# A gated linear attention and a bilinear feed-forward: the same steps in another written order

## The chip, the core and the metric

The kernel runs on one core of one Trainium2 chip. The metric is the device time of one execution in microseconds (us). Of the kernel before there are three runs: 193.24, 193.31 and 193.69 us, median 193.31. A profile was taken of one more execution.

A core has five engines with a queue of instructions each: TensorE (PE in the profile; its weight loads are listed as PEld), VectorE (DVE), ScalarE (ACT), GpSimd (POOL) and SyncE (SP). Each works through its own queue in order, and waits on semaphores for the others. DMA transfers are issued from a queue, here GpSimd's and SyncE's (and once ScalarE's), and run beside the engines. Memory on the core is SBUF, and PSUM for what TensorE writes.

## The reference

There are 4 batches, 8 heads, 768 positions and a head width of 48. The first half is a recurrence over the positions, with a gate alpha for each element:

```python
for t in range(S):
    state = alpha[:, :, t, :, None] * state + np.einsum('bhd,bhe->bhde', k[:, :, t], v[:, :, t])
    y[:, :, t] = np.einsum('bhd,bhde->bhe', q[:, :, t], state)
```

The result, seen as 3072 tokens of 384 values, goes through a bilinear feed-forward of inner width 1536:

```python
a = x @ w_a
b = x @ w_b
return (a * b @ w_out).astype(np.float32)
```

Inputs and output are float32.

## The kernel before

**Tiling.** The 768 positions are cut into three stretches of 256 and the four batches into two pairs: six *chunks*, numbered 0 to 5 (chunk c holds stretch c // 2 of batches c % 2 * 2 and the next). The two batches of a chunk are its *units* u = 0 and 1. A partition holds two neighbouring positions r = 0, 1, and the 128 partitions of a unit are two halves g = 0 and 1 of 64, between which a state is carried.

**The steps.** The kernel is a list of steps, `PROGRAM`, written out by hand or by a planner outside the kernel; an interpreter at its end calls one small function for each step, in the order of the list. Nothing reorders it later: the order of the list is, engine by engine, the order of each queue, and what a step waits for follows from the tiles and the PSUM banks that it touches. A line of the list begins with the chunk; the letter at a step's end names the engine where there is a choice: V VectorE, S ScalarE, P GpSimd, Y SyncE. A step's last number is mostly its PSUM bank, of eight (0 to 7); wide results take that bank and the next. The steps, in the order in which a chunk needs them:

- `ld a|k|q|v`: loads of alpha, k, q, v. `W a|b`, `Wo`: loads of the feed-forward's weights, in column pieces. `T`: a transposing DMA by SyncE of chunks 2 to 5's scaled q and k of a unit; `dr`, `dl`: the last gates of each half written out and read back by DMA. `st`, `stc`: stores of the output.
- `ln`: logarithm of alpha (ScalarE, line 510). `l2`, `l2s`: sum of it over a pair of positions. `H`, `L`, `R`: splits of that sum into parts for exact products. `B`, `A2`, `AQ`: the running sum over positions as matmuls (lines 545 and 546, 592, 587). `dk`, `de`: the sum over a half as matmuls (654) and its exponential. `ra`, `lv`: correction within a pair (599, 606).
- `E x i`, `E x b`: exponentials of the sum with both signs (621). `mk`, `mq`: k and q times them, into `QKp` (632).
- `C`, `Ce` (chunks 0 and 1): transposes on TensorE (692) and the copy of the result out of PSUM into `kqT` (914 on ScalarE, 916 on VectorE and GpSimd). `Tr` (chunks 2 to 5): a reordering copy of `T`'s keys into `kp`.
- `v`, `vs`: values copied into `vx`, once straight (725, 727) and once with their quarters of 32 partitions swapped. `vs u g e` makes the two copies of 32 x 384 elements of a unit's half g on engine e.
- `K`, `K2`: what keys and values add to the state (748, 761). `k`: the new state (775, or 778 and 779). `D`: the scores (793). `M` masks them out of PSUM on VectorE (802); `Mc` copies them on ScalarE (806) and `Mm` masks the copy on VectorE (810).
- `SB`, `SA`, `Y`: the output of the attention, from the carried state and from the masked scores (822). `X`: its copy to `xT` (858, 860).
- `a f w`, `b f w`: three matmuls (877) for block f of 12 of the feed-forward, over half of the chunk's tokens (w = 0 or 1; 256 columns) or all (`*`; 512). I call one such step a pass. `as`: `a` copied to SBUF by ScalarE (883). `pr`: times `b`, on VectorE (891), which frees both banks.
- `o m h`: half of the last product for 128 tokens (899), `oc` the same in smaller pieces (910). `ot`: its copy to SBUF (914 or 916), then `st`.

**What lies where.** GpSimd's queue holds loads between its other work, and waits of that work hold back the loads behind it. SyncE's queue holds loads, stores and `T` of chunks 2 to 5; a `T` that waits for VectorE holds back the loads behind it. Chunk c + 1's attention is laid between chunk c's feed-forward passes, so that TensorE has passes to do while the other engines prepare.

Of the kernel before, what the change touches and what calls it, by code (L numbers as in the profile page):

```python
# [17 lines left out]
0: cm 0; c1; cz 0 b P; ci; ld a 0b Y; c1a; ld a 0a Y; ln 0b; cu; cz 1 b P; fill 7 0; cu2 V; cz 0 q V; cus; ld k 0b Y; ld k 0a Y; B 0b 2; ln 0a  # L18
# [21 lines left out]
0: as 4 1; pr 4 1; pr 10 *; a 9 * 2; a 3 1 1; Wo 6 12  # L40
1: L 1 V
2: ld a * P
1: ld v 1 P; E 0 b
0: b 8 * 7
1: E 0 i
0: as 3 1; as 9 *
2: ld q * P
1: lv 0 k V; mk 0 V
0: b 3 1 1; pr 3 1
1: dk * 4; de *  # L50
0: b 9 * 1
# [72 lines left out]
1: a 5 1 5; pr 2 1; a 9 0 4; b 9 0 6; b 5 1 7; as 6 1; pr 6 1
2: lv 0 k P; mk 0 V; T 0
3: v 0 S
1: as 9 0; pr 9 0; a 3 1 1; b 3 1 3; as 5 1; pr 5 1
2: K2 * * 4 5
3: vs 0 0 V; ra 0
1: b 9 1 6; as 3 1  # L130
4: ld a * Y
1: pr 3 1; a 9 1 1; o 2 0 3; o 2 1 -
2: k * 0 V; k * 1 V
3: vs 0 1 S
0: st 1 Y
1: b 0 1 7
2: Tr 1 V; v 0 S; vs 0 1 V
3: ld q * Y
1: b 7 1 4; as 0 1; pr 0 1; as 9 1; as 1 1
3: ld k * Y  # L140
1: b 8 1 2; a 7 1 5; ot 2 S
2: v 1 S; vs 1 1 P
3: l2s 0 P
1: as 7 1
4: ld k * Y
3: v 1 V
1: pr 9 1; b 1 1 3; pr 1 1; pr 7 1; a 11 1 0
# [12 lines left out]
2: SB 0 0; SB 1 2; D 0 1 6; Mc 0 1; Mm 1 0 V  # L160
1: o 3 0 5; o 3 1 -
2: vs 1 0 S
3: AQ 6
2: SA 0
1: ot 3 S; st 3 Y
0: st 2 Y
3: E 1 b; E 0 b; dr
4: ld q * Y
3: dl
2: SA 1  # L170
3: E 1 i
# [885 lines left out]
```

## Time and profile before

| | us |
|---|---|
| median of three runs | 193.31 |
| the profiled execution | 193.74 |
| its span, first to last instruction | 191.8 |
| TensorE busy | 184.5 |
| VectorE busy | 136.8 |
| ScalarE busy | 114.1 |
| GpSimd busy | 52.9 |

A row of the timeline gives the start, the duration, the engine, the line, the operation, output<-inputs by the names of the program, the shapes and how many like instructions were merged; in brackets stands how long the engine had been idle and what ended that. A row of a group gives, behind the bar, the busy time, the mean duration in ns, and the idle time ahead of them. Matmuls are pipelined: a mean duration is longer than the time from one start to the next. Issuing a DMA is shown on the engine whose queue issues it (SPq is SyncE's queue).

### The profile page before, as it was taken

The numbers are of one execution on the slowest core, as the hardware profiler recorded it, in microseconds if no ns is written. First come the engines' busy times: TensorE is split into PE (matmuls) and PEld (weight loads), VectorE is DVE, ScalarE is ACT, GpSimd is POOL, SyncE is SP. The second block draws the span as 40 slices with busy tenths as digits, with TensorE's granted clock in tenths as the row PEclk, the third lists the DMA queues.
The fourth block names the chain that finished last, engine by engine and source line by source line (L and its number), as shares of the span: only waits on it lengthen the run. The fifth ranks groups of instructions, "written<-read, shape, count | busy, mean of one in ns | idle before, by whom it ended". The sixth has DMA issues, their size and how long they took to land.

```text
span 191.8 us, 6128 instructions
## 1 busy us (share of the span) xinstructions
PE 184.5 (96%) x2597; PEld 115.2 (60%) x2613; DVE 136.8 (71%) x251; ACT 114.1 (59%) x216; POOL 52.9 (28%) x80
## 2 busy tenths in 40 slices
PE   7999999999999999999999999999999999999993
PEld 3987775666778876644446554556446555444562
DVE  2398887888998997689899996899085742234711
ACT  4446475797988888853867558775266151424321
POOL 8999506595424035000460000300030000000000
PEclk9999999999999999999999999999999999999999
DMA  5999999999994999989999988026812100210013
GB/s 137 267 221 213 254 249 239 241 265 269 252 207 86 84 205 281 257 240 156 200 296 191 180 123 201 4 82 86 177 6 82 46 3 0 82 41 3 0 68 137
DMA packets 64475, 29.41 MB, mean 153 GB/s; under 512 B 55760, under 2 KB 62816, under 8 KB 64448
## 3 DMA queue, kind: packets, MB, share of 16 engines
q1 hardware_dynamic: 46080, 16.34, 40.3%
q0 software_dynamic: 18224, 12.58, 38.0%
q8 instruction: 20, 0.33, 0.7%
q10 hardware_dynamic: 144, 0.10, 0.1%
q14 instruction: 7, 0.06, 0.1%
HBM read 25.98 MB, written 4.74 MB: 160 GB/s over the span
## 4 chain that ended last, share of the span: by engine, by line
PE 73%; DVE 12%; DMA 5%; issue 3%; ACT 3%; SPq 2%; DVEq 0%; ACTq 0%
PE psum L877 38%; PE psum L899 18%; DMA k_t<-in_k_dram 5%; PE psum L822 4%; DVE QKp L632 2%; DVE prod L891 2%; PE psum L528 2%; PE psum L692 2%; DVE vx L916 2%; PE psum L793 2%; SPq L932 1%; PE psum L748 1%; PE psum L545 1%; PE psum L910 1%; PE psum L546 1%
## 5 line engine op out<-in xcount | busy, mean ns | idle before, releaser
L877 PE MATMUL psum<-xT,wa_t 128*128 128x512 bf16 (+1 forms) x265 | 55.0, 336 | 0.6 <-DVE tmp L778 0.2
L877 PE MATMUL psum<-xT,wb_t 128*128 128x512 bf16 (+1 forms) x260 | 54.5, 335 | 0.9 <-DVE prod L891 0.3
L899 PE MATMUL psum<-wo_t,prod 128*128 128x384 bf16 x276 | 49.4, 326 | 0.0
L877 PEld LDWEIGHTS <-wa_t 128*128 128x128 bf16 x270 | 25.8, 98 | 20.6 <-issue 0.8
L877 PEld LDWEIGHTS <-wb_t 128*128 128x128 bf16 x270 | 25.5, 98 | 19.3 <-issue 0.9
L899 PEld LDWEIGHTS <-prod 128*128 128x128 bf16 x276 | 26.2, 98 | 17.6
L916 POOL COPY vx<-v_t 32x384 bf16<-32x384 bf16 x12 | 6.1, 508 | 49.8 <-ACT vx L725 40.9
L914 ACT ACTIVATE ot<-psum 128x384 f32<-128x384 f32 (+1 forms) x19 | 9.0, 472 | 11.3 <-PE psum L899 9.7
L806 ACT ACTIVATE m<-psum 128x768 bf16<-128x768 f32 x14 | 11.0, 810 | 2.9 <-PE psum L793 2.9
L606 POOL TENSOR_TENSOR q_t<-q_t,ra 128x384 f32<-128x384 f32 x4 | 4.0, 998 | 30.8 <-ACT ra L599 21.0
L916 DVE COPY ot<-psum 128x384 f32<-128x384 f32 x6 | 3.3, 557 | 11.2 <-PE psum L899 11.2
L510 ACT ACTIVATE la<-a_t 128x1536 f32<-128x1536 f32 (+2 forms) x9 | 9.5, 1054 | 2.9 <-DMA a_t<-in_alpha_dram 2.9
L858 ACT ACTIVATE xT<-psum 128x768 bf16<-128x768 f32 x10 | 7.9, 809 | 4.3 <-PE psum L822 4.3
L802 DVE TENSOR_TENSOR m<-psum,mask 128x768 bf16<-128x768 f32 x10 | 9.3, 951 | 1.3 <-PE psum L793 1.3
L632 DVE TENSOR_TENSOR QKp<-q_t,beta 128x768 bf16<-128x768 f32 x10 | 9.5, 954 | 0.6 <-DVE q_t L606 0.5
L632 DVE TENSOR_TENSOR QKp<-k_t,invb 128x768 bf16<-128x768 f32 x10 | 9.4, 953 | 0.2
L822 PE MATMUL psum<-m,vx 64*64 64x64 bf16 (+1 forms) x576 | 8.7, 205 | 0.2 <-issue 0.2
L503 POOL DMA_DIRECT2D v_t<-in_v_dram x8 | 8.5, 1063 | 0.0
L822 PEld LDWEIGHTS <-vx 64*64 64x64 bf16 x576 | 7.5, 108 | 0.6 <-issue 0.5
L725 ACT ACTIVATE vx<-v_t 128x768 bf16<-128x768 bf16 x9 | 7.6, 843 | 0.0
L822 PE MATMUL psum<-kqT,Sm 64*64 64x128 bf16 x144 | 7.6, 218 | 0.0
L914 ACT ACTIVATE vx<-v_t 32x384 bf16<-32x384 bf16 x14 | 7.3, 522 | 0.2
(278 smaller groups left out, 308.6 us busy)
## 6 DMA issues: line engine op xcount, KB each, us to landing
out_dram<-ot SPq DMA_DIRECT2D x23, 192.0 KB, 2.1
q_t<-in_q_dram SPq DMA_DIRECT2D x3, 768.0 KB, 6.2
k_t<-in_k_dram SPq DMA_DIRECT2D x3, 768.0 KB
a_t<-in_alpha_dram POOLq DMA_DIRECT2D x2, 768.0 KB, 11.3
v_t<-in_v_dram POOLq DMA_DIRECT2D x4, 384.0 KB, 11.1
a_t<-in_alpha_dram SPq DMA_DIRECT2D x2, 768.0 KB
a_t<-in_alpha_dram POOLq DMA_DIRECT2D x3, 384.0 KB, 7.8
k_t<-in_k_dram POOLq DMA_DIRECT2D x3, 384.0 KB, 6.9
```

The lines of the kernel that those rows point to most:

```text
L503: eng.dma_start(out=t[:, us, hs].rearrange("p b h r d -> p (b h) (r d)"), in_=src[ch.b0 + us.start:ch.b0 + us.stop, hs, ch.s * 2 * C:(ch.s ...
L510: nc.scalar.activation(out=ch.la[:, us, hs].rearrange("p b h r d -> p (b h r d)"), in_=ch.a[:, us, hs].rearrange("p b h r d -> p (b h r d) ...
L632: eng.tensor_mul(QKp[ch.c % 2][:, u, j, :, hs, :D], src[:, u, hs].rearrange("p h r d -> p r h d"), f)
L725: nc.scalar.activation(out=o_, in_=i_, func=AF.Copy)
L802: nc.vector.tensor_mul(m, x, maskn())
L806: nc.scalar.activation(out=m, in_=x, func=AF.Copy)
L822: nc.tensor.matmul(o, lhsT=lhsT, rhs=rhs, start=(g, c) not in begun, stop=False, skip_group_check=True)
L858: nc.scalar.activation(out=o_, in_=i_, func=AF.Copy)
L877: nc.tensor.matmul(p, lhsT=(wa_t, wb_t)[w][:, kk, f * 128:(f + 1) * 128], rhs=ch.xT[:, kk, us, :], start=(kk == 0), stop=(kk == KT - 1))
L899: nc.tensor.matmul(op, lhsT=ch.prod[:, f, at:at + C], rhs=wo_t[:, f, :], start=(f == 0), stop=(f == NFF - 1))
L914: nc.scalar.activation(out=o_, in_=i_, func=AF.Copy)
L916: eng.tensor_copy(o_, i_)
```

## The change

The list holds the same 872 steps, and each queue issues the same loads. What differs is the order of the steps, the PSUM banks, and the engine of 45 of them. By engine, the swaps `vs` go from 11 on VectorE, 7 on ScalarE and 6 on GpSimd to 10, 11 and 3. GpSimd issues its loads in the old order. On SyncE the loads keep their order among themselves, and some stores stand elsewhere between them. `l2 0` of chunk 1 moves from VectorE to GpSimd, `Ce 0 1` of chunk 0 from VectorE to ScalarE, `Ce 0 0` and `Ce 1 1` of chunk 1 the other way, and some `lv`, `v`, `Tr`, `ot` and `X` change engine in both directions. The work on each engine in all stays nearly as it is.

The start of the list, chunk 0 and the first steps of chunk 1:

```diff
-0: B 0a 0; ld q 0b Y; E 0b i; mk 0b V; dk 0 4; E 0b b; mq 0b V; C 0 1 5; E 0a i; mk 0a V; E 0a b; fill 2 0; ld v 0 P; ld q 0a Y; mq 0a V; de 0; Ce 0 1 V; ld a 1 P
-0: ln 1; cs 0 m P; C 0 0 1; Ce 0 0 V; ld k 1 P; K 0 0 2; k 0 0 V; ld q 1 P; cm 1; D 0 1 4; M 0 1; D 0 0 0; M 0 0; v 0 S; vs 0 1 V; SB 0 2; vs 0 0 V; B 1a 6
-0: E 1a b; mq 1a V; E 1a i; mk 1a V; B 1b 4; W b 0 256; E 1b b; mq 1b V; dk 1 0; E 1b i; de 1; C 1 0 1; cz 0 v P; Y 0; SA 0; mk 1b V; C 1 1 0; Ce 1 0 V
-0: Ce 1 1 V; D 1 0 4; ld v 1 P; K 1 0 1; K 1 1 6; X 0 S; v 1 S; Mc 1 0; D 1 1 2; Mc 1 1; W a 256 768; a 3 0 0; a 4 0 7; k 1 0 V; cz 1 q P; as 4 0; vs 1 0 V; a 5 0 1
-0: W a 0 256; a 0 0 4; as 5 0; vs 1 1 V; Mm 1 0 V; SB 1 2; W b 256 768; b 4 0 5; Mm 1 1 V; cs 1 m P; b 3 0 1; a 1 0 7
-1: ld a 0 P; ld a 1 P
-0: k 1 1 V; a 2 0 6; as 2 0; pr 4 0; K 0 1 5; k 0 1 V; SA 1; Y 1; b 2 0 6; pr 2 0; b 1 0 5; as 1 0; pr 1 0; b 5 0 7; pr 5 0; W a 768 1536; X 1 S; c2 P
-0: b 2 1 2; a 2 1 3; W b 768 1536; a 1 1 5
...
+0: ln 0a; ld v 0 P; E 0b i; mk 0b V; E 0b b; mq 0b V; B 0a 0; E 0a i; ld q 0a Y; ld a 1 P; dk 0 2; cs 0 m P; ld k 1 P; ld q 1 P; E 0a b; cm 1; W b 0 256; C 0 1 3
+0: Ce 0 1 S; fill 2 0; mk 0a V; cz 0 v P; ld v 1 P; mq 0a V; C 0 0 1; Ce 0 0 V; K 0 0 0; W a 256 768; de 0; D 0 1 2; cz 1 q P; D 0 0 4; W a 0 256; W b 256 768; ln 1; cs 1 m P
+1: ld a 0 P
+0: k 0 0 V; v 0 S; vs 0 0 S; M 0 1; SB 0 0; B 1a 6
+1: ld a 1 P
+0: M 0 0; vs 0 1 V; B 1b 2; E 1a b; W a 768 1536; mq 1a V; dk 1 4; E 1a i; mk 1a V; C 1 0 5; c2 P; Y 0; SA 0; W b 768 1536
+1: ld q 0 P
+0: E 1b i; mk 1b V; K 1 0 6; E 1b b; v 1 S; mq 1b V; C 1 1 7
+1: ld k 0 P; ld v 0 P
+0: Ce 1 0 V; D 1 0 2; K 1 1 5; X 0 S; a 3 0 0; vs 1 0 V; de 1; Mc 1 0; as 3 0; a 4 0 4; as 4 0; a 5 0 1; Ce 1 1 V; k 1 0 V; D 1 1 2; k 1 1 V; SB 1 6; vs 1 1 V
+0: a 1 0 0; Mm 1 0 V; b 4 0 4; pr 4 0; Mc 1 1; a 2 0 5; as 2 0; Mm 1 1 V
+1: ln 0
+0: b 3 0 2; a 0 0 3; b 2 0 5
+1: l2 0 P
+0: b 5 0 4; pr 3 0; as 5 0; pr 5 0; SA 1; Y 1; X 1 S; pr 2 0; K 0 1 2; b 0 0 1
 1: ld q 1 P
...
+0: b 1 0 4; a 3 1 5; a 2 1 6; Wo 0 6; b 2 1 7; as 0 0
```

Further on, the places in SyncE's queue of `T 0` of chunk 2, a store of chunk 0 and the loads behind them, and VectorE's steps around chunk 2's `Y`s:

```diff
+0: st 1 Y
...
+2: lv 0 k P; mk 0 V; T 0
...
+4: ld a * Y
...
+3: ld q * Y; ld k * Y
...
-2: lv 0 k P; mk 0 V; T 0
...
-4: ld a * Y
...
-0: st 1 Y
...
-3: ld q * Y
...
-3: ld k * Y
...
-2: SB 0 0; SB 1 2; D 0 1 6; Mc 0 1; Mm 1 0 V
-1: o 3 0 5; o 3 1 -
-2: vs 1 0 S
-3: AQ 6
-2: SA 0
...
-3: E 1 b; E 0 b; dr
...
-2: Mm 0 0 V; Mm 0 1 V; Y 1; X 1 V
...
-2: Y 0; X 0 S
+1: o 3 1 -; ot 3 S; st 3 Y
+2: Mm 1 0 V
+3: R 1
+2: vs 0 1 V; Mm 0 0 V
+3: AQ 6; E 0 b
+2: SA 0; vs 1 0 V; Y 1
+3: E 1 b
+2: vs 0 0 V
...
+2: Mm 0 1 V; Y 0; SA 1
+3: lv 0 q V; mq 0 V
...
+2: X 0 S
...
+2: X 1 S; a 3 * 7; b 0 * 2
```

In the last 60 us the passes, `T` and `dr` of chunk 5 stand in another order too; the last four `oc` groups and the last stores stand in the same order.

More of the change, by code (lines that the diff above doesn't have):

```diff
@@ L47 @@
+1: H 0 V; L 0 V; ra 0
+0: b 0 1 3; pr 0 0; as 1 0; pr 1 0
+1: ln 1; ra 1
+0: k 0 1 V
+1: l2 1 V; H 1 V; L 1 V
+0: as 2 1; a 0 1 0; as 0 1; as 3 1; b 3 1 1; a 6 * 4
+1: A2 0 2; E 0 i
+0: pr 0 1
+1: lv 0 q P
+0: pr 2 1; b 1 1 0
+1: ld k 1 P
+0: a 10 * 5; Wo 6 12; as 6 *
+2: ld a * P
+0: a 7 * 6; pr 3 1; b 6 * 3; pr 6 *; b 10 * 1; as 10 *; pr 10 *
+1: E 0 b; mq 0 V
+0: b 7 * 7; as 7 *; pr 7 *
+1: ld v 1 P; dk * 2
+0: a 1 1 1
 2: ld q * P
+1: lv 1 q P; lv 1 k P; de *
+2: ld k * P
 1: lv 0 k V; mk 0 V
-0: b 3 1 1; pr 3 1
@@ new lines @@
+3: ld v * P
+0: cz 1 v P; b 11 * 3; a 4 1 5; as 1 1; as 11 *; pr 11 *; a 5 1 1
+1: A2 1 2
+0: pr 1 1
+1: E 1 i
+0: b 8 * 6
+1: E 1 b
+0: b 4 1 4; c3 P
+3: ld a * P
+1: mq 1 V; v 0 S
+0: a 8 * 7
+1: C 0 0 0; Ce 0 0 V
+0: b 5 1 2; o 2 0 3; as 5 1; as 4 1; pr 4 1; cs 1 0 P; as 8 *
+1: vs 0 0 S; C 0 1 7; D 0 0 0
+0: pr 5 1; pr 8 *
+1: K2 0 0 2 4; k 0 0 V
+0: o 3 0 5
+1: Mc 0 0; mk 1 V; Ce 0 1 S; vs 0 1 S
+0: o 1 0 2
+1: k 0 1 V; SB 0 0
+2: ln *
+1: D 0 1 6
+0: o 3 1 -
+1: M 0 1; Mm 0 0 V; v 1 S; C 1 0 4; Ce 1 0 V; C 1 1 6; Ce 1 1 V
@@ new lines @@
+3: vs 0 0 S
+1: b 4 1 2
+2: Tr 0 V
+1: b 11 1 3; o 0 0 0; pr 4 1
+2: D 1 0 4; Mc 1 0; D 0 0 6; Mc 0 0
+1: b 1 1 1; o 0 1 -; pr 11 1
+3: R 0
+2: SB 1 2; SB 0 4; D 0 1 6
+1: pr 1 1; o 3 0 1
+2: Mc 0 1
+1: o 3 1 -; ot 3 S; st 3 Y
[6 more added lines that the diff above has]
+2: vs 0 0 V
+0: st 2 Y; cs 0 0 P
+2: Mm 0 1 V; Y 0; SA 1
+3: lv 0 q V; mq 0 V
+1: o 1 0 1; o 1 1 -
+3: E 1 i; lv 0 k V
+2: X 0 S
+3: lv 1 q V; mq 1 V
+2: X 1 S; a 3 * 7; b 0 * 2
@@ L196 @@
+3: E 0 i
+4: ln *; ra 1; l2 0 P
+2: b 1 * 3
+3: dr
+2: a 0 * 6; as 0 *
+1: ot 1 S
+3: lv 1 k V; mk 1 V
+2: a 1 * 4; b 11 * 5
+3: mk 0 V
+4: ld q * Y
+1: ot 0 S
+2: pr 0 *; b 3 * 6; as 3 *
+3: v 1 V; vs 1 0 V
+4: l2s 0 V
+2: as 1 *; pr 1 *
+3: dl
+2: pr 3 *; a 6 * 0; a 11 * 1; a 7 * 4
+3: K2 * * 2 7
+2: as 11 *
+3: k * 0 V; k * 1 V
+1: st 2 Y
+2: pr 11 *; b 9 * 1; a 5 * 3
+3: vs 0 1 S
+2: as 5 *
+3: T 0
+2: a 2 * 6; b 2 * 2; as 2 *; pr 2 *; b 5 * 3; pr 5 *
 3: T 1
-4: lv 0 k V
-2: as 3 *; as 4 *; pr 4 *; a 9 * 2; as 9 *; b 9 * 5
+2: a 4 * 6
@@ L355 @@
-5: oc 1 0 1 -; otc 1 0 S; stc 1 0 Y
+2: b 10 * 1; pr 10 *
+3: D 0 1 2
+4: lv 0 q P
+3: Mc 0 1
+4: lv 1 q V
+3: D 0 0 4; Mc 0 0; D 1 0 6; M 1 0; Mm 0 1 V
+2: o 0 0 0; o 0 1 -
+3: SB 1 2; SB 0 4
+4: l2s 1 P
+3: D 1 1 6; Mc 1 1
+2: o 2 0 1; o 2 1 -
+5: ln *
+3: Mm 0 0 V
+2: ot 2 S
+4: R 0; R 1; AQ 6; E 0 b; E 1 i; lv 1 k V
+3: Mm 1 1 V
+5: l2s 0 V
+4: mq 0 V
+3: vs 1 1 P
+4: E 0 i
+3: SA 1; SA 0; Y 0; X 0 S; Y 1; X 1 S
+4: E 1 b
+5: l2 0 V
+2: st 2 Y
+1: st 1 Y
+2: o 1 0 1; o 1 1 -
+4: lv 0 k P; mk 0 V
@@ new lines @@
+5: l2s 1 V; R 0
+3: a 2 * 2
+4: mq 1 V
+3: as 2 *; b 9 * 3
+4: ld v * P
+5: R 1; ra 1
+4: T 0
+3: a 8 * 4; as 8 *
+4: dr
+3: b 2 * 2
+4: v 0 V; mk 1 V
+3: a 4 * 5; as 4 *; a 9 * 4
+4: T 1; v 1 S; vs 1 0 S
+3: b 4 * 6; pr 4 *; b 8 * 5; pr 8 *; pr 2 *
+5: lv 1 q V
+3: b 11 * 7
+4: Tr 0 V
+3: a 6 * 6; as 6 *; b 6 * 5; pr 6 *
+2: ot 1 S
+5: ra 0
+3: as 9 *
+5: lv 0 q P
+3: a 11 * 2; as 11 *; pr 9 *
+2: ot 0 V
+3: a 1 * 6; pr 11 *; b 1 * 1; as 1 *; pr 1 *
+4: vs 1 1 S
+3: a 3 * 4; b 3 * 5; as 3 *; pr 3 *; a 5 * 0; as 5 *
@@ new lines @@
+5: lv 0 k P; AQ 2; E 0 b; E 0 i
+4: dl
+5: ld v * P
+4: D 0 1 6; vs 0 1 P; K * 0 1; D 0 0 4; M 0 0; k * 0 V; Tr 1 S
+2: st 1 Y
+4: vs 0 0 S
+5: E 1 b
+4: M 0 1
+2: o 3 0 0; o 3 1 -; ot 3 S
+3: b 5 * 2; pr 5 *
+5: mk 0 V; mq 0 V
+3: a 7 * 1
+5: dr
+4: D 1 1 4; SB 0 6
+5: E 1 i
+4: Mc 1 1
+3: a 0 * 0
+5: lv 1 k V
+3: b 0 * 2; as 0 *; pr 0 *; b 7 * 3; a 10 * 0
+4: D 1 0 4
+3: as 7 *
+4: Y 0; Mc 1 0; SB 1 1; SA 0
+3: pr 7 *; b 10 * 3
+5: mq 1 V; mk 1 V
+3: o 0 0 4
+5: T 0
+3: as 10 *; pr 10 *
+5: Tr 0 V
@@ new lines @@
+3: o 3 0 0; o 1 0 3
+5: T 1
+3: o 0 1 -
+5: K * 0 5
+4: Mm 1 0 V; Mm 1 1 V; Y 1; SA 1; X 1 V
+5: dl
+3: ot 0 V; o 1 1 -; o 3 1 -
+4: X 0 S; a 6 * 1; as 6 *; b 6 * 2; a 3 * 4
+5: k * 0 V; Tr 1 S
+4: pr 6 *
+2: st 3 Y
+4: a 0 * 1; as 0 *; as 3 *
+3: ot 3 V
+4: a 4 * 2; b 3 * 0; pr 3 *
+3: o 2 0 1
+5: D 0 0 4; D 1 0 6; v 1 V; M 1 0
+2: st 0 Y
+3: ot 1 S
+5: vs 1 1 V
+4: as 4 *
+5: D 1 1 2; vs 1 0 S
+4: b 0 * 0
+3: o 2 1 -
+5: v 0 S; vs 0 1 P
+3: ot 2 S
+5: vs 0 0 V; Mc 0 0; Mm 0 0 V
+4: b 9 * 6
+5: Mc 1 1
```

376 lines of the change are left out of this document (93 added, 283 removed).

## The prediction

> **What bounds the kernel now.** I read the page first: its head, the slices and the shares of the chain.
>
> ```profile
> span 191.8 us, 6128 instructions
> PE 184.5 (96%) x2597; PEld 115.2 (60%) x2613; DVE 136.8 (71%) x251; ACT 114.1 (59%) x216; POOL 52.9 (28%) x80
> ...
> DVE  2398887888998997689899996899085742234711
> ...
> PEclk9999999999999999999999999999999999999999
> ...
> PE 73%; DVE 12%; DMA 5%; issue 3%; ACT 3%; SPq 2%; DVEq 0%; ACTq 0%
> ```
>
> TensorE is busy for 96% of the span at full granted clock. Both orders issue the same matmuls, so the change can move only what TensorE waits for: some idle time before the first matmul, and holes that VectorE's results, ScalarE's results or late loads leave. VectorE is at eight to nine tenths up to about the thirtieth slice (140 us) and slack afterwards, so I looked for holes in the first 100 us, by the timeline of each engine and the chain of waits. I compare the orders by landmarks: a place where equally much TensorE work lies behind. A pass is three matmuls with one weight block; a half-wide one (256 columns) takes 0.33 us in the timeline below (1.48 us for twelve matmuls, four passes, less the pipelined tail).
>
> **The change, part one: the start.** The stretch from 10 to 26 us, from the timelines of ScalarE, VectorE and TensorE:
>
> ```profile
> 10.50 0.84 ACT L510 ACTIVATE la<-a_t 128x768 f32<-128x768 f32 x1 [0.87 <-DMA a_t<-in_alpha_dram]
> 11.25 0.83 ACT L725 ACTIVATE vx<-v_t 128x768 bf16<-128x768 bf16 x1
> 13.63 0.87 ACT L621 ACTIVATE prod<-psum 128x384 f32<-128x384 f32 x2 [1.55 <-PE psum L546]
> 15.78 0.35 ACT L675 ACTIVATE bl<-psum 48x8 f32<-48x8 f32 x2
> ```
> ```profile
> 9.84 1.50 DVE L916 COPY kqT<-psum 128x1024 bf16<-128x1024 bf16 x2
> ...
> 11.51 1.81 DVE L802 TENSOR_TENSOR m<-psum,mask 128x768 bf16<-128x768 f32 x2
> 13.36 1.42 DVE L916 COPY vx<-v_t 32x384 bf16<-32x384 bf16 x4
> 14.80 0.56 DVE L632 TENSOR_TENSOR QKp<-q_t,prod 128x384 bf16<-128x384 f32 x1
> 15.28 0.55 DVE L632 TENSOR_TENSOR QKp<-k_t,prod 128x384 bf16<-128x384 f32 x1
> ...
> 18.97 1.71 DVE L916 COPY vx<-v_t 32x384 bf16<-32x384 bf16 x4
> ```
> ```profile
> 14.82 0.91 PE L654 MATMUL psum<-og,la 128*48 128x2 f32 x32
> 15.89 0.62 PE L692 MATMUL psum<-ident,QKp 128*128 128x128 bf16 x8 [0.15 <-DVE QKp L632]
> 16.44 0.72 PE L822 MATMUL psum<-m,vx 64*64 64x128 bf16 x48
> ...
> 22.80 0.49 PE L748 MATMUL psum<-v_t,QKp 64*64 64x48 bf16 x16 [0.26 <-DVE prod L891]
> ...
> 23.92 1.48 PE L877 MATMUL psum<-xT,wb_t 128*128 128x256 bf16 x12
> 25.24 0.82 PE L877 MATMUL psum<-xT,wa_t 128*128 128x256 bf16 x6
> ```
> ```profile
> L914 ACT ACTIVATE vx<-v_t 32x384 bf16<-32x384 bf16 x14 | 7.3, 522 | 0.2
> L916 DVE COPY vx<-v_t 32x384 bf16<-32x384 bf16 x22 | 6.6, 298 | 0.4
> ...
> L914 ACT ACTIVATE kqT<-psum 128x1024 bf16<-128x1024 bf16 x3 | 3.1, 1029 | 0.0
> ```
>
> The last fence is the list of groups by form: a swap is two copies, so 1.04 us on ScalarE and 0.60 on VectorE.
>
> ScalarE in the new order takes over `Ce 0 1` at 9.84 (1.03, to 10.87), then `de 0` (0.35, to 11.22), the logarithm (0.84, to 12.06), the cast (0.83, to 12.89), the swap (1.04, to 13.93) and the first exponential of 1a (half of 0.87, to 14.37), some 0.3 us later than now. VectorE has one swap instead of two: 13.32 plus half of 1.42 is 14.03; it waits for that exponential, and the two products of 1a end near 15.50 (0.48 us from start to start in the rows). TensorE's gate sums end at 15.73 (14.82 + 0.91), so the transposes `C 1 0` can start there, not at 15.89. The order after it (`Y 0`, `SA 0`, `K 1 0`, `C 1 1`) keeps TensorE fed while VectorE makes the products of 1b and `Ce 1 0`.
>
> The larger gain is at 22 us. Now the pass at 22.06 ends in 0.5 us, and `K 0 1` waits until 22.80 for bank 5 (`pr 4 0`). In the new order `K 0 1` stands behind `SA 1` and `Y 1`, with seven half-wide passes ahead of them; I followed each bank and found its `as` or `pr` done before it is asked for, `pr 4 0` by 0.4 us. That gives: `SB 1` done near 20.1, seven passes 2.3, `SA 1` and `Y 1` 0.9, `K 0 1` 0.3, two passes 0.65, together 24.25. Equal work lies before 25.24 now. Gain 1.0 us; I take 0.9, with ends 0 (ScalarE's chain 0.3 us later than reckoned at several places) and 1.2.
>
> Where copies run beside loads I used 0.85 us a pair (half of 1.71), not 0.52, the undisturbed pair:
>
> ```profile
> 48.86 0.52 DVE L916 COPY vx<-v_t 32x384 bf16<-32x384 bf16 x2
> ```
>
> The Trainium skill ("SBUF — State Buffer", Who interferes with whom) says that VectorE's fast copies and GpSimd contend for one port pair, which whoever starts first holds for its whole instruction while the other stands still. The 0.85 against 0.52 agrees with a copy that loses. If each copy waited out a load's whole issue (0.89 us in a row below), `vs 1 0`, which the new order puts ahead of `Ce 1 1` on VectorE, would cost 1.8 + 0.5 us instead of 0.85; `D 1 1` would be that much later, the start's gain would be gone, and the sum below would be some 193.3.
>
> GpSimd's queue: `l2 0` (about 1 us) now stands ahead of `ld q 1` and `Wo 0 6` and waits for ScalarE's logarithm, so these two loads go out near 24.5 and 25.4, not at the 20.45 and 21.90 of these rows.
>
> ```profile
> 20.45 0.89 POOL L503 DMA_DIRECT2D q_t<-in_q_dram  x1
> 21.90 0.82 POOL L486 DMA_DIRECT2D wo_t<-in_moe_w_out_dram  x1 [0.56 <-DMA a_t<-in_alpha_dram]
> 30.46 1.00 POOL L606 TENSOR_TENSOR q_t<-q_t,ra 128x384 f32<-128x384 f32 x1 [7.73 <-DMA q_t<-in_q_dram]
> ```
> ```profile
> 20.00:30.00 10.00, 9.52 (x138) 7.16 (x138) 8.09 (x21) 6.29 (x15) 2.05 (x3) 1.00 1.12 241
> 40.00:50.00 10.00, 10.00 (x231) 6.64 (x229) 9.23 (x20) 8.54 (x13) 5.78 (x7) 1.00 1.22 255
> 50.00:60.00 10.00, 9.87 (x156) 7.57 (x155) 9.49 (x17) 8.90 (x21) 3.52 (x4) 1.00 1.12 175
> ...
> 70.00:80.00 10.00, 10.00 (x265) 6.94 (x263) 7.28 (x14) 8.95 (x16) 4.46 (x7) 1.00 1.21 264
> ```
>
> These windows list PE, PEld, DVE, ACT and POOL, the clock, the DMA share and GB/s. From 20 to 30 us the transfers run at 241 GB/s with a share over 1, that is with a backlog, and GpSimd stands idle 7.73 us until the q load issued before these lands. The cover is that backlog: cost 0, and up to 4 us later loads if it were gone.
>
> **Part two: chunk 1 and the sums for chunk 2 (38 to 57 us).** VectorE is full here (9.23 and 9.49 of 10 us) and sets the pace. The new order takes `vs 0 1`, `v 1` and the pair sum off it ahead of `AQ`, and puts `Ce 0 0`, `Ce 1 1` and `ot 3` on it: in rows of this kind (0.5, 0.35, 0.55 against 0.7, 0.7, 0.56) about even, half a microsecond more. It also places `k 1 0` and `R 1` nearer to when they are asked for. I take 0, ends a gain of 0.6 and a loss of 0.6.
>
> **Part three: chunk 3's loads (64 to 87 us).** SyncE's queue, then VectorE and TensorE:
>
> ```profile
> 64.44 1.82 SPq L701 DMA_TRANSPOSE kqT<-QKp  x1
> 66.43 1.00 SPq L503 DMA_DIRECT2D a_t<-in_alpha_dram  x1
> 67.48 2.20 SPq L932 DMA_DIRECT2D out_dram<-ot  x1
> 69.78 0.38 SPq L503 DMA_DIRECT2D q_t<-in_q_dram  x1
> 70.27 7.42 SPq L503 DMA_DIRECT2D k_t<-in_k_dram  x2
> ```
> ```profile
> 85.39 1.83 DVE L632 TENSOR_TENSOR QKp<-k_t,invb 128x768 bf16<-128x768 f32 x2
> ```
> ```profile
> 87.28 0.70 PE L761 MATMUL psum<-v_t,QKp 64*64 64x48 bf16 x64 [0.42 <-DVE QKp L632]
> ```
>
> The k load of chunk 3 goes out behind a store that holds the queue for 2.20 us; `K2` waits 0.42 us for the last two products made from it. The new order puts this store (`st 1`) ahead of `T 0`, whose own wait for VectorE covers it, so q and k go out about 2.2 us earlier, and `K2` stands two full passes (1.3 us) later in TensorE's order. The wait goes: a gain of 0.4, ends 0 and 0.6. What is late next is VectorE, part four. `3: dr` and `ld q 4` move behind more of ScalarE's and VectorE's work; `q 4` is needed only in `lv 0 q`, some 10 us on, so 0.
>
> **Part four: VectorE between chunk 2's scores and its `Y`s (68 to 82 us).** `vs 1 0` comes from ScalarE and `vs 0 0` from GpSimd, `vs 0 1` stands later; `lv 0 q` (0.5) and `mq 0` (0.95) come forward. That is 1.8 us of swaps and 1.5 of products, 3.3 us, in a stretch in which VectorE now has 2.7 us free (7.28 of 10). In order of need the swaps and `Mm`s stand ahead of `lv` and `mq`; counted from the end of `K2` with the rows' durations, `Mm 0 1` is ready 0.3 us before `Y 0` is reached. I take a loss of 0.2, ends 0 and 3.3.
>
> **The rest.** How long loads take to land, of all rows of the load line:
>
> ```profile
> DMA to landing us min/median/max: 4.1/9.2/13.5
> ```
>
> Chunk 5's `T`, `dr` and loads move forward by several microseconds; its `lv`s on GpSimd (1.0 us each) stand ahead of `ld v` for chunk 5, which goes out some 15 us of TensorE work before `K` asks for it, more than the longest landing of 13.5: 0. In the last 60 us no engine beside TensorE is full, and the last `oc` groups and stores stand in the same order: 0.
>
> **Sum.** −0.9 + 0 − 0.4 + 0.2 = −1.1 us. The profiled execution took 193.74 us (span 191.8 and 1.9 around it), 0.43 above the median 193.31: it would go to 192.6, the median to 192.2. Ends: −2.4 and +3.3 or so.
>
> **Rivals.** (a) VectorE becomes the bound in part four. Its work there waits on `K2`, `D` and `Mc`, so it can't run ahead into the free time; the block of 3.3 us then pushes `Y 0`, `Y 1` and every pass of chunk 2 by 2.3 to 3.3. For it: the eight and nine tenths of the slices on both sides; against it: the order of need. It decides once the loss exceeds the 1.3 us gained elsewhere; at 2.5 the time is 193.3 − 1.3 + 2.5 = 194.5. Chance 0.22. (b) The lead is given back: landings are set by the backlog, not by TensorE, and a TensorE that is 0.9 us ahead finds chunk 2's alpha and chunk 3's k no earlier. Then only the wait of 0.4 at most goes: 193.1 to 193.4. For it: 241 to 255 GB/s up to 50 us; against it: the passes between landings that TensorE has in hand. Chance 0.14. (c) The copies lose a whole issue each: 193.3 as worked out above, chance 0.03. (d) More than the sum goes, as VectorE's part two gains too: 191.0 to 191.4. Chance 0.11.
>
> **The numbers.** The forecast, 192.2 with its own range 191.4 to 192.9, has 0.50. From 0.3% (0.58 us, what a measurement here can tell from no change) the cases give: faster, 0.46 of the forecast's 0.50, and (d), 0.57; same, the remaining 0.04, (b), (c), 0.21; slower, (a), 0.22. The range goes from (d)'s 191.0, just below, to (a)'s 194.5: 190.9 to 194.6.
>
> **What would show it.** Right: twelve half-wide passes, `Y 1` and `K 0 1` are behind TensorE by 24.5 us; no wait of TensorE for `pr` at 22; chunk 3's k load issued before 69 us; no wait before chunk 3's `K2`; span near 190.7. Wrong: TensorE waiting for `vx` or `m` at chunk 2's `Y`s; ScalarE's exponentials of 1b after 16.5; waits for `la` of chunk 2; GpSimd's next load after `Wo 0 6` much later than 31.4.

## The result

| | before | after |
|---|---|---|
| median | 193.62 us (11 runs) | 192.01 us (11 runs) |
| range | 192.32 to 194.38 | 191.62 to 193.29 |
| ratio, 95% interval | | 0.9938 [0.9917, 0.9958] |
| again, beside other runs | 193.43 us (23 runs) | 191.72 us (6 runs) |
| ratio, 95% interval | | 0.9922 [0.9896, 0.9948] |
| span of the profiled run | 191.8 us | 190.6 us |

By the ratios after is faster by 0.6 to 0.8%, that is 1.2 to 1.5 us; the medians lie 1.6 and 1.7 us apart. 192.2 had been predicted, and a span near 190.7. The steps of the prediction fared worse than its sum, as the profile shows. First the page of after: span, busy times, VectorE's slices, the shares of the chain.

```profile
span 190.6 us, 6117 instructions
PE 182.8 (96%) x2599; PEld 113.4 (60%) x2613; DVE 137.5 (72%) x250; ACT 117.7 (62%) x221; POOL 52.0 (27%) x76
...
DVE  2479687888999799789899988894757652454420
...
PE 86%; POOL 6%; DMA 5%; issue 1%; DVE 0%; ACT 0%; POOLq 0%
```

VectorE had 12% of the chain and has none of it now. DMA has 5% in both, but for another transfer: it was chunk 3's k before, and it is a piece of the weights `wb` now. The next two fences give that transfer's place: TensorE's timeline of after, then three pieces of its chain between 8 and 26 us (start, duration, what).

```profile
19.51 0.50 PE L874 MATMUL psum<-xT,wa_t 128*128 128x256 bf16 x3
21.86 0.50 PE L874 MATMUL psum<-xT,wb_t 128*128 128x256 bf16 x3 [1.84 <-DMA wb_t<-in_moe_w_b_dram]
...
24.64 0.41 PE L745 MATMUL psum<-v_t,QKp 64*64 64x48 bf16 x16
24.98 0.83 PE L874 MATMUL psum<-xT,wb_t 128*128 128x256 bf16 x6
25.72 0.49 PE L874 MATMUL psum<-xT,wa_t 128*128 128x256 bf16 x3
```
```profile
12.29 0.69 POOL wa_t L480
12.98 8.83 DMA wb_t<-in_moe_w_b_dram
21.81 0.05 issue
```

The new order reaches its first `b` of blocks 2 to 5 at 20.0 us, but columns 256 to 768 of `wb` land at 21.81. `K 0 1` starts at 24.64, and the place with equal work behind it is reached at 25.72, where it was 25.24 before.

To find where the 1.2 us come from I use one number at several places. The *lag* is the start of a step's first matmul less the TensorE work in front of it in the order, where each matmul counts the undisturbed time from one start to the next of its kind (215.7 ns for 512 columns, 108.7 for 256, 162.7 for `o`, and so on). All orders hold the same work, 179.64 us by this count; what the lag grows by was waiting or slow clock. The weight of the small matmuls is an estimate, so the level of a lag depends on it; differences between two kernels at the same work are good to about 0.1. In us, at so much work done:

| kernel | 6 | 21 | 66 | 78 | 99 | end |
|---|---|---|---|---|---|---|
| before | 2.67 | 5.09 | 6.78 | 6.92 | 8.52 | 8.87 |
| after | 1.43 | 5.56 | 6.72 | 6.78 | 7.40 | 7.77 |
| after, a second profile | 2.07 | 4.68 | 6.06 | 6.13 | 6.72 | 7.09 |
| new_start | 1.35 | 4.56 | 5.95 | 6.01 | 7.32 | 7.67 |
| st1_early | 2.14 | 4.62 | 6.01 | 6.07 | 7.11 | 7.46 |
| k2_late | 2.06 | 5.08 | 6.57 | 6.64 | 8.43 | 8.78 |
| tr1_early | 1.42 | 4.97 | 6.59 | 6.65 | 7.68 | 8.14 |
| x1_scalar | 1.85 | 4.23 | 6.24 | 6.31 | 7.41 | 7.76 |
| fill_wait | 2.23 | 4.39 | 5.62 | 5.73 | 6.53 | 6.90 |
| fill_again | 2.79 | 4.69 | 5.81 | 6.41 | 7.06 | 7.55 |

The first column is not the order's doing. Timeline of the first running sums, of before and then of after:

```profile
4.92 0.85 PE L546 MATMUL psum<-la,uts 128*128 128x192 f32 x2
...
6.84 0.52 PE L545 MATMUL psum<-la,ut 128*128 128x192 f32 x2
7.20 0.49 PE L546 MATMUL psum<-la,uts 128*128 128x192 f32 x2
```
```profile
4.15 0.68 PE L542 MATMUL psum<-la,ut 128*128 128x192 f32 x2
4.66 0.49 PE L543 MATMUL psum<-la,uts 128*128 128x192 f32 x2
```

The same matmuls take twice as long from start to start until 7.0 us in the one and only until 4.5 in the other, and the profiles with these two starts lie anywhere between, whichever start they have. By 21 us of work the lead of 1.2 us that after had has gone in waits for loads, and it is 0.5 behind. So two profiles alone can't be subtracted; the growth from 21 on can.

### The profile page after: what moved, and what is told of

It is laid out like the page before. It is cut to its first block, busy times and chain, and to the rows that moved or that the text cites. A ratio compares the mean times of both kernels' runs of the same rounds, so it can differ in the third digit from the quotient of the medians.

```text
span 190.6 us, 6117 instructions
## 1 busy us (share of the span) xinstructions
PE 182.8 (96%) x2599; PEld 113.4 (60%) x2613; DVE 137.5 (72%) x250; ACT 117.7 (62%) x221; POOL 52.0 (27%) x76
## 4 chain that ended last, share of the span: by engine, by line
PE 86%; POOL 6%; DMA 5%; issue 1%; DVE 0%; ACT 0%; POOLq 0%
PE psum L874 49%; PE psum L896 24%; PE psum L819 5%; DMA wb_t<-in_moe_w_b_dram 5%; PE psum L790 2%; PE psum L584 1%; PE psum L907 1%; POOL v_t L500 1%; PE psum L689 1%; PE psum L758 1%; POOL mask L456 1%; POOL wa_t L480 1%; PE psum L745 1%; POOL q_t L500 0%; POOL a_t L500 0%
## 5 line engine op out<-in xcount | busy, mean ns | idle before, releaser
L874 PE MATMUL psum<-xT,wb_t 128*128 128x512 bf16 (+1 forms) x263 | 56.3, 336 | 2.2 <-DMA wb_t<-in_moe_w_b_dram 1.8
L874 PE MATMUL psum<-xT,wa_t 128*128 128x512 bf16 (+1 forms) x264 | 56.0, 336 | 0.5
L911 ACT ACTIVATE ot<-psum 128x384 f32<-128x384 f32 (+1 forms) x17 | 7.9, 472 | 10.3 <-PE psum L896 9.2
L603 POOL TENSOR_TENSOR q_t<-q_t,ra 128x384 f32<-128x384 f32 x5 | 5.0, 1009 | 31.1 <-ACT ra L596 26.5
L911 ACT ACTIVATE vx<-v_t 32x384 bf16<-32x384 bf16 x22 | 11.5, 521 | 0.8 <-DVE vx L724 0.4
L515 POOL TENSOR_TENSOR l<-la 128x384 f32<-128x384 f32 x3 | 3.0, 1012 | 27.4 <-ACT la L507 27.4
L913 DVE COPY ot<-psum 128x384 f32<-128x384 f32 x8 | 4.4, 552 | 7.0 <-PE psum L896 7.0
L913 POOL COPY vx<-v_t 32x384 bf16<-32x384 bf16 x6 | 3.1, 518 | 23.2 <-ACT vx L722 23.0
L807 DVE TENSOR_TENSOR m<-m,mask 128x768 bf16<-128x768 bf16 x14 | 8.0, 584 | 0.9 <-ACT m L803 0.8
L819 PE MATMUL psum<-m,vx 64*64 64x128 bf16 (+1 forms) x576 | 8.4, 205 | 0.0
```

The lines of the kernel that those rows point to most:

```text
L807: eng.tensor_mul(m, m, maskn())
L819: nc.tensor.matmul(o, lhsT=lhsT, rhs=rhs, start=(g, c) not in begun, stop=False, skip_group_check=True)
L874: nc.tensor.matmul(p, lhsT=(wa_t, wb_t)[w][:, kk, f * 128:(f + 1) * 128], rhs=ch.xT[:, kk, us, :], start=(kk == 0), stop=(kk == KT - 1))
L911: nc.scalar.activation(out=o_, in_=i_, func=AF.Copy)
```

## Experiments

Every kernel here does all 872 steps. Four splice the two orders, five move one to three steps of before or give one to another engine, one mends after, and two repeat.

**The new start, then before's order.**

```diff
-0: b 0 0 6
-1: ln 0; l2 0 V; ld k 0 P
-0: a 0 1 7
-1: ld v 0 P
-0: as 0 0; pr 0 0
...
+0: a 1 0 0; Mm 1 0 V; b 4 0 4; pr 4 0; Mc 1 1; a 2 0 5; as 2 0; Mm 1 1 V
+1: ln 0
+0: b 3 0 2; a 0 0 3; b 2 0 5
+1: l2 0 P
+0: b 5 0 4; pr 3 0; as 5 0; pr 5 0; SA 1; Y 1; X 1 S; pr 2 0; K 0 1 2; b 0 0 1
...
```

Up to here it is the list of after; all steps behind stand in the order of before.

> The list of steps of after up to its step 129 (about 25.6 us, where the first passes of chunk 0 are under way), then every step that is left in the order, on the engines and in the banks of before (one bank moved). It tells what the new start is worth alone. The prediction on record (the start gives 0.9 us, the rest 0.2): 0.9 below before. The reading of the two traces (in after TensorE waits 1.84 us at 20 us for the weights wb, columns 256 to 768, and is 0.4 to 0.5 behind at equal work from there on): 0.4 above before, and the wait of about 1.8 us for wb in the profile. Third, the reading that the lead at the start was only a clock that rose earlier in that execution: near before, within 0.3.

Measured: 192.87 against 193.04 us, ratio 0.9996 [0.9969, 1.0022]. The wait is there, and was shorter as the transfer landed at 20.67 (TensorE's timeline):

```profile
20.71 0.50 PE L879 MATMUL psum<-xT,wb_t 128*128 128x256 bf16 x3 [0.84 <-DMA wb_t<-in_moe_w_b_dram]
```

The start alone gains nothing that can be measured: the interval ends at a gain of 0.6 and a loss of 0.4 us, so the 0.9 of the record is out. Over all profiles with before's start (eight, the splices below and x1_lvq among them) the lag at 21 us of work is 4.76 on average, over four with after's start 4.94. That is less than single profiles of one start differ (4.23 to 5.09 in the table with before's), and three us of work later the difference is gone.

Before's start waits for the same transfer in most executions. TensorE's first pass with these weights in before, and in tr1_early below, whose start is the same:

```profile
20.73 0.83 PE L877 MATMUL psum<-xT,wb_t 128*128 128x256 bf16 x6
```
```profile
21.33 0.83 PE L876 MATMUL psum<-xT,wb_t 128*128 128x256 bf16 x6 [0.90 <-DMA wb_t<-in_moe_w_b_dram]
```

In six of the eight profiles with before's start, this pass begins 0.04 to 0.05 us after the transfer has landed, in four of them after a listed wait of 0.2 to 0.9. In before it had landed at 20.16, earlier than in any other profile.

**Before's start, then after's order.**

The list is that of before up to this place, and from here on it has after's order:

```diff
-0: a 0 1 7
-1: ld v 0 P
-0: as 0 0; pr 0 0
+1: ld v 0 P
+0: as 3 0; pr 3 0
+1: ld q 1 P
+0: a 3 1 7; Wo 0 6; as 0 0
...
```

> The other way round: before up to its step 131 (about 26.4 us), then the steps left in the order of after (18 banks moved). It tells what the change is worth without its start. The prediction on record: 0.2 below before. The reading of the traces: after less the 0.4 to 0.5 that its start loses, 1.5 below before, with no wait for wb and, if that holds, faster than after by 0.4.

Measured: 194.6 us, ratio 1.0077 [1.0051, 1.0103], slower. TensorE waits 1.05 us at 27.8 for ScalarE's `as` and 1.09 at 51.2 for `xT`, at places where neither kernel waits: steps that after has done early stand in a heap behind the joint, and 18 banks had to be changed. It says nothing on what the rest is worth.

**The splice at 79 us, both ways.**

At the `o 1 0` of chunk 1 the one list goes over to the order of the other; first after that goes on as before, then before that goes on as after:

```diff
-3: lv 0 q V; mq 0 V
-1: o 1 0 1; o 1 1 -
...
+3: lv 0 q V; mq 0 V; vs 0 1 S; v 1 V
+4: ln *
+3: dr
...
+1: o 1 0 5; o 1 1 -; ot 0 S
```
```diff
-1: o 1 0 5; o 1 1 -
...
+3: lv 0 q V; mq 0 V
+1: o 1 0 1; o 1 1 -
+3: lv 0 k V; lv 1 q V; mq 1 V
+2: a 3 * 7; b 0 * 2
```

> After up to its step 451 (the first o of chunk 1's third group, 79.4 us), then the steps left in the order of before. The prediction on record (0.9 gained at the start, 0.2 lost around chunk 2's Y): 0.7 below before. The reading of the traces (lag behind TensorE's work 6.89 against 7.03 there): 0.1 below before, within its interval.

> Before up to its step 460 (the same o, 79.6 us), then the steps left in the order of after (12 banks moved). The prediction on record (only chunk 3's K2 wait of 0.4 lies behind): 0.4 below before. The reading of the traces (the lag grows from 7.0 to 8.9 in before and from 6.9 to 7.8 in after): 0.9 to 1.0 below before, most of the whole change, and no wait at chunk 3's K2, scores and Y.

Measured: 197.02 us, ratio 1.0193 [1.0147, 1.0239], and 194.52 us, ratio 1.0081 [1.0055, 1.0107]. Both expectations missed, and again by waits at the joint for a late `xT`: 2.90 and 0.92 us. The first showed something else. TensorE's timeline, then windows as in the prediction (PE, PEld, DVE, ACT, POOL, granted clock, DMA):

```profile
82.07 4.00 PE L897 MATMUL psum<-wo_t,prod 128*128 128x384 bf16 x12 [2.90 <-ACT xT L856]
```
```profile
80.00:82.00 2.00, 0.00 (x0) 0.00 (x0) 1.51 (x3) 2.00 (x4) 0.00 (x0) 0.80 1.21 313
82.00:84.00 2.00, 1.93 (x7) 0.90 (x7) 1.97 (x4) 0.78 (x3) 0.00 (x0) 0.50 0.49 128
...
88.00:90.00 2.00, 2.00 (x11) 0.93 (x10) 0.00 (x0) 0.86 (x2) 0.00 (x0) 0.99 1.15 216
```

During 2.9 us without a matmul the granted clock falls to 0.50, and it stays there for 6 us of the work that follows, so the one wait costs its 2.9 us about twice. These splices don't tell the parts of the change from each other; single steps had to.

**Part three's store alone.**

```diff
+0: st 1 Y
 2: T 0
...
-0: st 1 Y
```

> Before with one step moved: the store st 1 of chunk 0 ahead of T 0 of chunk 2 in SyncE's queue. This is what the prediction's part three gives its 0.4 us to. The prediction on record: the k load of chunk 3 goes out 2.2 us earlier (near 68 us), TensorE's wait of 0.42 before chunk 3's K2 goes, 0.4 below before. The reading of the traces (in after the store stands ahead, and yet the k load goes out at 70.26, as in before, and the first product of it starts at 80.78 against 80.83): the landing moves by less than 0.5 us, the wait stays, time as before within 0.2.

Measured: 193.24 against 193.22 us, ratio 0.9984 [0.9958, 1.001]. SyncE's queue in new_start, which has the old order here and the same lag, and in st1_early; then TensorE in st1_early:

```profile
66.95 1.58 SPq L934 DMA_DIRECT2D out_dram<-ot  x1
68.62 0.38 SPq L505 DMA_DIRECT2D q_t<-in_q_dram  x1
69.11 7.49 SPq L505 DMA_DIRECT2D k_t<-in_k_dram  x2
```
```profile
67.00 1.52 SPq L504 DMA_DIRECT2D q_t<-in_q_dram  x1
68.62 7.80 SPq L504 DMA_DIRECT2D k_t<-in_k_dram  x2
```
```profile
86.32 0.70 PE L762 MATMUL psum<-v_t,QKp 64*64 64x48 bf16 x64 [0.32 <-DVE QKp L633]
```

Without the store ahead of it the q load takes 1.52 us to issue where it took 0.38. Whatever stands behind `a` takes long here: the store 1.58 and, in before, 2.20 us, the q load 1.52 and, in after, 1.64. Why isn't shown. The k load goes out 0.5 us earlier, not 2.2, and the wait stays.

**Part three's K2 alone.**

```diff
-3: K2 * * 2 3; k * 0 V
...
 2: b 4 * 4; a 4 * 1
+3: K2 * * 2 3; k * 0 V
 2: a 0 * 5
```

> Before with chunk 3's K2 (and the first state step on VectorE behind it) moved two full passes later in TensorE's order, and nothing else. Both the prediction and the reading of the traces: the wait of 0.42 for the last product goes, 0.4 below before. If it doesn't go, the products themselves came late in after's place for another reason (a copy of xT and a pair sum that before has on VectorE ahead of them).

Measured: 193.92 against 193.22 us, ratio 1.0029 [1.0006, 1.0052], slower, where both readings had 0.4 us faster. TensorE, then VectorE:

```profile
87.51 0.81 PE L878 MATMUL psum<-xT,wb_t 128*128 128x512 bf16 x3 [0.94 <-DVE prod L892]
...
88.90 0.70 PE L762 MATMUL psum<-v_t,QKp 64*64 64x48 bf16 x64
```
```profile
85.00 1.83 DVE L633 TENSOR_TENSOR QKp<-k_t,invb 128x768 bf16<-128x768 f32 x2
86.74 0.72 DVE L892 TENSOR_TENSOR prod<-as__1887,psum 128x512 bf16<-128x512 bf16 x1
```

The wait before `K2` is gone, and a wait of 0.94 stands at the pass that takes its place: its bank is freed by a product that VectorE makes after the same two products of k. VectorE was late, not `K2` early.

**VectorE lightened ahead of chunk 3's products.**

```diff
-2: X 1 V
+2: X 1 S
```

> Before with one step on another engine: X 1 of chunk 2 (0.96 us on VectorE at 79.13, just ahead of chunk 3's products) by ScalarE, as in after; order unchanged. If VectorE's queue sets the last product before chunk 3's K2: products 0.6 to 0.9 earlier, the wait of 0.4 goes, 0.4 below before. If the landing of chunk 3's k does (the first product that uses it starts within 0.2 us of the landing in before): VectorE only waits longer for it, the products end where they did, the wait of 0.3 to 0.4 stays, time as before.

Measured: 193.04 against 193.43 us, ratio 0.9993 [0.9972, 1.0014]. VectorE at the landing, then TensorE:

```profile
80.14 0.56 DVE L606 TENSOR_TENSOR k_t<-k_t,a_t 128x384 f32<-128x384 f32 x1 [2.26 <-DMA k_t<-in_k_dram]
```
```profile
86.22 0.70 PE L761 MATMUL psum<-v_t,QKp 64*64 64x48 bf16 x64
...
92.36 1.46 PE L877 MATMUL psum<-xT,wa_t 128*128 128x512 bf16 x6 [0.16 <-ACT as__2003 L883]
```

VectorE now idles 2.26 us for k's landing, as the landing's reading has it, and yet the wait before `K2` is gone, as the queue's has it: the 0.48 us pause between the products (82.33 in before) went with it. The end is no earlier, as other waits follow some 6 us on.

```diff
-2: X 1 V
+2: X 1 S
+3: lv 0 q V; mq 0 V
 4: l2s 0 V
...
-3: lv 0 q V; mq 0 V
```

> The run before it with one thing more: chunk 3's lv 0 q and mq 0 (1.5 us on VectorE), which need no k, ahead of l2s 0 and of the first step that waits for k's landing, as in after. Expected by the landing's reading: VectorE does them while it waits, the last product ends 1.0 to 1.5 us earlier, the wait before K2 goes, and the passes behind it find prod done: 0.4 to 0.6 less lag of TensorE behind K2 than in x1_scalar. By the queue's reading: no more than 0.1 less than x1_scalar.

Measured: 193.34 against 193.43 us, ratio 1.0001 [0.997, 1.0032]. The last product ends at 85.25, some 1.4 us earlier against TensorE's work than in x1_scalar; that buys nothing more, for ScalarE is next:

```profile
93.03 1.46 PE L878 MATMUL psum<-xT,wa_t 128*128 128x512 bf16 x6 [0.45 <-ACT as__2003 L884]
```

**A copy moved off the v loads.** In before, GpSimd, VectorE and TensorE at 97 us:

```profile
96.68 2.35 POOL L503 DMA_DIRECT2D v_t<-in_v_dram  x2
```
```profile
97.15 0.96 DVE L916 COPY kp<-kqT 128x1024 bf16<-128x1024 bf16 x1
```
```profile
98.79 0.81 PE L877 MATMUL psum<-xT,wb_t 128*128 128x512 bf16 x2 [0.27 <-DVE prod L891]
```
```diff
+3: Tr 1 V
 2: pr 1 *
...
-3: Tr 1 V
```

> Before with one copy on VectorE moved: Tr 1 of chunk 3 (the keys' reordering, 0.96 us at 97.15 beside GpSimd's issue of two v loads from 96.68 to 99.03) two products earlier, ahead of that issue. If the copy is dearer because it runs beside the loads: it takes about 0.42 us as it does alone, TensorE's wait of 0.27 for prod behind it goes, and 0.3 to 0.5 are gained. If its length has another cause (its source, its bank), it still takes 0.9 and the wait stays or moves. The prediction on record put this stretch at 0.

Measured: 193.38 against 193.22 us, ratio 0.9993 [0.9969, 1.0017]. The same three in tr1_early:

```profile
96.21 2.35 POOL L502 DMA_DIRECT2D v_t<-in_v_dram  x2
```
```profile
96.07 0.48 DVE L915 COPY kp<-kqT 128x1024 bf16<-128x1024 bf16 x1
```
```profile
98.00 0.82 PE L876 MATMUL psum<-xT,wb_t 128*128 128x512 bf16 x2
```

The move is past one product of VectorE. Started ahead of the load's issue, the copy takes 0.48 us, and TensorE's wait behind it is gone (lag from 87 to 96 us of work: +0.22, against +0.60 in before and +0.53 in new_start). In after the copy takes 0.41 at 97.58, when the only v load there (96.20 to 97.39) is through. The Trainium skill ("SBUF — State Buffer", Who interferes with whom) says that VectorE's fast copies and GpSimd exclude each other from one port pair, for the whole instruction of whoever was first. The trace agrees for the copy: 0.5 us longer behind a load whose issue had begun, almost nothing ahead of it. The loads' issue takes 2.35 us in both, so for GpSimd's side this case shows nothing. The 0.3 us that TensorE gains is below what the whole time can show.

**The wait for wb filled.**

```diff
-0: a 1 0 0; Mm 1 0 V; b 4 0 4; pr 4 0; Mc 1 1; a 2 0 5; as 2 0; Mm 1 1 V
+0: a 1 0 0; Mm 1 0 V; Mc 1 1; b 1 0 4; as 1 0; Mm 1 1 V; pr 1 0; a 2 0 5; a 0 0 2; b 3 0 3; pr 3 0; as 2 0; b 4 0 4; pr 4 0; as 5 0
...
```

> After with the order of chunk 0's first half-wide passes changed: b 1 0, a 2 0 and a 0 0, whose weights have landed by then, stand ahead of the first pass that needs wb's columns 256 to 768 (the wait of 1.84 us in after's profile, 0.84 in two others with the same start). Same loads, same engines. Reading of the traces: TensorE asks for these weights 1.0 us later, the wait shrinks by that (to 0 to 0.9) and 0.8 are gained against after, 2.0 below before. Rival (b) of the prediction, landings set by the backlog and not by TensorE: the lead is given back at the next late landing (wa or wb, columns 768 to 1536, or chunk 1's alpha), and the time is after's, 1.2 below before.

> After, unchanged, beside the next run and on the same chip. 1.2 below before, as measured. Its profile tells how much of the wait for wb at 20 us (1.84) and of the clock at the first matmuls is this order and how much the execution: by the reading, a wait of 0.8 to 1.8 again, and a first full-rate matmul anywhere between 4.2 and 7.0 us.

> The order of fill_wait, unchanged, timed beside after on the same chip: 0.3 to 0.6 below after (191.76 against 192.01 so far, on different chips), wait for wb under 0.4.

Measured: fill_wait 191.76 us, ratio to before 0.9904 [0.9874, 0.9933]; side by side, after 191.72 us and fill_again 191.85 us, 0.9928 [0.9899, 0.9956]. TensorE in the second profile of after and in fill_wait:

```profile
20.78 0.50 PE L874 MATMUL psum<-xT,wb_t 128*128 128x256 bf16 x3 [0.68 <-DMA wb_t<-in_moe_w_b_dram]
```
```profile
20.78 0.49 PE L876 MATMUL psum<-xT,wb_t 128*128 128x256 bf16 x3
21.68 1.03 PE L876 MATMUL psum<-xT,wb_t 128*128 128x256 bf16 x8 [0.41 <-DVE prod L890]
```

The wait for `wb` is gone, and one for VectorE's `pr 1` stands a pass later. At 24 us of work the lag is 4.40 and 4.70 in the two, 4.69 in after's second profile: little or no lead is left. Not faster than after; the 0.3 to 0.6 expected did not come. After's own wait, expected at 0.8 to 1.8, was 0.68 this time. An order that also spares VectorE there was not tried, so whether the wait can be had for nothing stays open.

## Why the prediction came out right

The number held by luck: the gain foretold for the start did not come, and gains put at 0 came elsewhere. (The ends of the sum, too, add up to +3.9 and not to the +3.3 given there; nothing hangs on it.)

**Part one (−0.9) failed.** The step that failed is "seven half-wide passes ahead of them": I followed banks and engines, but not the landing of their weights. The transfer (columns 256 to 768 of `wb`) lands between 20.16 and 21.81 us in the fourteen profiles, and the new order asks at 20.0. Before asked at 20.73, after its landing at 20.16, so the one profile read for the prediction showed no wait; six of the eight with this start begin at the landing. A start that asks 0.7 us earlier then gains nothing. The hole at 22 us that was to be closed is no constant either: a wait of `K 0 1` for `pr` is listed in before and x1_lvq, the two of the eight that did not begin at the landing, and in none of the six others. Start alone: ratio 0.9996, and no difference in the lag beyond the spread. Rival (b) had the mechanism (landings aren't set by TensorE), but at chunk 2's alpha and chunk 3's k, and at 0.14. The sign that was to show it right, `K 0 1` behind TensorE by 24.5, came at 25.05 (24.64 + 0.41).

**Part two (0) was low.** From 21 to 66 us of work the lag grows by 1.12 to 1.38, 1.20 on average, in five profiles with after's order (new_to_79 is the fifth), and by 1.39 to 2.01, 1.57 on average, in eight with before's: 0.35 gained, within the ends of 0.6. Part of it lies before 24 us of work; counted from there the gain is 0.2.

**Part three (−0.4) had the size and not the cause.** No wait stands before chunk 3's `K2` in after. But the k load went out at 70.26 where "before 69 us" was foretold, and VectorE waits for it longer than before (0.80 against 0.15), having less to do until then. SyncE and VectorE of after:

```profile
65.15 2.66 SPq L698 DMA_TRANSPOSE kqT<-QKp  x1
...
68.53 1.64 SPq L500 DMA_DIRECT2D q_t<-in_q_dram  x1
70.26 3.57 SPq L500 DMA_DIRECT2D k_t<-in_k_dram  x1
```
```profile
80.78 0.56 DVE L603 TENSOR_TENSOR k_t<-k_t,a_t 128x384 f32<-128x384 f32 x1 [0.80 <-DMA k_t<-in_k_dram]
...
84.63 1.83 DVE L629 TENSOR_TENSOR QKp<-k_t,invb 128x768 bf16<-128x768 f32 x2 [0.48 <-DVE k_t L603]
```

k is used from 80.78; the same step in before:

```profile
80.83 0.56 DVE L606 TENSOR_TENSOR k_t<-k_t,a_t 128x384 f32<-128x384 f32 x1 [0.15 <-DMA k_t<-in_k_dram]
```

So k lands no earlier. Neither the store nor `K2`'s place does it alone (st1_early, k2_late). The products end at 86.46 instead of 87.22, since `X 1` is ScalarE's and `mq 0` is done ahead of the landing; the first of these takes the wait away by itself (x1_scalar).

**Part four (+0.2) cost nothing.** From 66 to 78 us of work the lag grows by 0.06 in after and 0.14 in before: the order of need held, and rival (a) with its 194.5 did not come.

**The rest (0) held more of the gain.** From 78 to 99 us of work the two unmended profiles of before's order (before, new_start) grow by 1.60 and 1.31, the four of after's by 0.62, 0.59, 0.80 and 0.65: about 0.8 less in after's order, 0.3 to 0.4 of it the wait of part three (the lag at `K2`: +0.59 and +0.49 against +0.21 twice). Of the rest, the copy beside the v loads is 0.3 (tr1_early). Up to 0.3 more is no gain of the order. It is a stall inside the `Y 0` of chunk 3 (0.38 in before, 0.29 in new_start), for which the profile names no other engine and which comes and goes: st1_early and x1_scalar, with the same order there, have 0.01, and fill_again has 0.5 at chunk 2's `Y 1`. Its place is a count. In the nine profiles that have such a stall, of 0.2 to 0.6 us, it falls ahead of about the 350th, the 1245th or the 1630th matmul of the list, whichever step that is (in old_to_79 the last of these belongs to `SA 0`). These places are 895 and 383 matmuls apart, close to 7 and 3 times 128. The page of the profile lists a queue of kind instruction, here in before; k2_late has the stall inside `K 0 1`, near the 350th matmul:

```profile
q8 instruction: 20, 0.33, 0.7%
```
```profile
23.02 0.27 PE L749 MATMUL psum<-v_t,QKp 64*64 64x48 bf16 x5 [0.52 <-issue]
```

Twenty transfers and 0.33 MB for 2613 matmuls are 16 KB for about 130 matmuls and their weight loads. Each time, TensorE goes on 1.3 to 1.7 us after such a transfer has ended. So TensorE most likely waits for its own instructions there; no run tests it. Without the stall the 0.8 is 0.4 to 0.5: st1_early, which has before's order and the wait of part three but not the stall, grows by 1.04. Behind 99 us nothing differs: 0.35 in before, 0.37 in after.

So the start gives about 0, part two 0.2 to 0.35 and what lies behind it 0.4 to 0.5 without the stall: 0.6 to 0.9 of the 1.2 to 1.5 measured. The splits are good to some 0.2 each, since each kernel has few profiles, and what is left is not placed. That the gain lies behind the start is shown by new_start; how it divides there is read from lags alone, since no run takes a part of the change out of after. That no single step of parts three and the rest moves the whole time, while all together do, fits what k2_late, x1_lvq and fill_wait show: behind each wait stands the next engine. That an order must ease VectorE and ScalarE at once to keep the gain follows from this, but no run shows it; what the swaps by ScalarE alone are worth was not tried.

## What to carry to other kernels

Before a step is drawn forward, look up the landing of every transfer that it reads, in more than one profile: a lead in TensorE's queue ends at the first one. When a wait names an engine, moving the waiting step can, as here, only pass the wait to the next user of that engine; take work off the engine, and look who is late next. Compare two profiles by the growth from a common place on, not by their spans, when the first microseconds differ from run to run.

## What was unexpected of the hardware

- The first running sums go to full rate at 4.5 us in one execution and at 7.0 in another, with the same steps ahead of them (after 4.5, its second profile 5.6). The Trainium skill ("TensorE: Matmul & The Clock Gate", Part 1) has the rate double after a window of activity that runs free and isn't reset by the kernel; the spread of 2.5 us fits in its window of about 3.4, but is more than the 0.5 us either way that the same section gives for the change from run to run. The granted clock of the profile reads 1.00 all through these microseconds, so only the times from start to start show the change.
- Within the kernel, a wait of 2.90 us went with a granted clock of 0.50 for 6 us behind it (new_to_79); one of 1.84 (after) left it at 1.00.
- Taking a store from ahead of two loads on SyncE made the first load's issue longer (0.38 to 1.52 us) and brought the second out 0.5 us earlier, where the store had held the queue for 1.58.
- A stall of 0.2 to 0.6 us without a waiting engine comes back at the same count of matmuls, in orders that have other steps there, and only in some executions.
